# Prefix products by one scan, weight parts by copies and adding transfers, and a new order of all engines in a fused Mamba-2 and SiLU kernel

## The chip, the core and the metric

The kernel runs on one core of one Trainium2 chip. The engines of the core each work through their own queue in order: PE multiplies matrices (PEld loads the weights that stand in it), DVE is the vector engine, ACT the scalar engine, POOL the general one, and SP issues most of the DMA transfers; ACT and POOL can issue transfers too. The metric is the device time of one execution in microseconds (us), the median of several runs.

## What is computed

An attention block of the Mamba-2 kind for 4 batches, 8 heads, 768 positions, head dimension 32 and state size 16, and behind it a feed-forward block on its 3072 rows of 256 numbers:

```python
cum = np.cumsum(log_a[chunk])                       # log_a = log(clip(a))
L = np.exp(cum[:, None] - cum[None, :]) * causal    # decay between positions
y_intra = ((C @ B.T) * L) @ x                       # per chunk and head
y_inter = (C @ state) * np.exp(cum)
state = np.exp(cum[-1]) * state + (B * np.exp(cum[-1:] - cum)).T @ x
...
x = y.transpose(0, 2, 1, 3).reshape(3072, 256)
h = x @ w_in                                        # 256 x 2048
g = h * (1.0 / (1.0 + np.exp(-h)))
out = g @ w_out                                     # 2048 x 256
```

Everything is float32.

## The kernel before

**Tiling.** The positions are cut into 12 units of 256 (three for each batch), a unit into four chunks of 64. Two units make a group of 512 rows, 0 to 5. W_in and W_out are cut into 16 blocks of 256: blocks 0 to 7 are columns of W_in, block 8 + i holds the rows of W_out that belong to block i.

**Order.** Nothing is scheduled by a program: `SCHEDULE` is a long list of tokens written out by hand. A token such as `q,1,4,1,1` is a name with its arguments; the table `DO` maps the name to a function that records one step, and the loop at the end of the kernel runs the tokens one after the other. Each engine gets its instructions in the order of the list. `SLOTS` says, in the same way by hand, which buffer of the pools s2k (128 x 512), r4k (128 x 1024), raw (128 x 1024) and hp (matrix results) each new tile takes.

**Weights.** `lw,n` loads block n (512 KB, L288). ACT makes `u` and `v` of it (L294, L297), DVE does three bit operations `w,n,0` to `w,n,2` (L303, L307, L310), and POOL adds the two into the block `W` (L318). In group 0 the blocks 0 to 5 of W_in (`s`, L696) and all of W_out (`n1`, L760) are multiplied in plain float32. All else uses three float32r parts: high `H` (ACT, L322), low `lD` = H + W (DVE, L326), third `dD` = Z times H plus low (DVE, L330); the functions are `w_high`, `w_low` and `w_third`. The activations get three parts too: `xh`, `x,u,0`, `x,u,1` for W_in and `h`, `l`, `e` for W_out. Matmuls of W_in are `a` (high and low, 8 matmuls) and `d` (third part, 4; both L799), those of W_out `q` (3; L781), with `q,P,i,k,m` for group P, block 8 + i, half k of its rows and half m of the columns.

**Attention.** For a unit: `E` forms the decays by two scans (DVE, L511), `T` transposes C or B (DVE, L524; for units 0 and 1 `tp` on PE, L530, does a part), `ce` splits C by odd and even heads with the mask `par` (ACT, L545), `B` and `C` scale B and C (POOL, L519 and L550; `C,1` and `C,2` on DVE), `g0` (L584) and `gd` (L570) multiply, `M` masks (DVE, L599), `b` copies (ACT, L593), `S` and `SM` carry the state (DVE L612 and L614, ACT L622), `Y` multiplies (PE, L634 and L643), `y` copies, `xh` and `x` split. `par` is made by `cP`, two reductions of a constant (DVE, L419). Units 0 and 1 get their a, decays and prefix products from small loads of their own (`ia`, `ip`, `P01`, `as`, `ab`).

**Prefix products.** `C` and `S` need, for each chunk, the running product of a with a 1 in front, 65 numbers for each of 8 heads. For units 2 to 11 `ir` loads all of a (48 chunks as partitions), `AA` clips it on POOL into `azt` and `acp`, `AD,4` writes azt to DRAM as `az` (L465) and `AD,0` to `AD,3` write acp to DRAM as `ac`, one batch each (L467). `La` reads az back, spread for the decays (ab). `Lp,u` reads ac back, spread over 16 partitions a head, into `pz` (L237), and `P,u` makes the products of it with one DVE scan (L483) into `pfx`.

**Names in the profile.** Tiles keep the program's names: s2k and r4k are the pools; ga and gb are the two matrix result buffers of attention and of `a` and `d`; hp and o_ps are the others; raw also holds the split activations of groups 1 to 5.

Of the kernel before, what the change touches and what calls it, by code (L numbers as in the profile page):

```python
# [28 lines left out]
Ln,2,1,1,0 ir,2 w,11,0 AA,0 tp,2 AD,4 H,7 lD,7 u,8 lw,13 w,8,0 w,8,1 u,13 w,13,0 lw,6 u,15 H,3 Lt,3,0,0,0 u,6 w,6,0
w,13,1 H,2 s,1,4 w,15,0 w,15,1 s,0,1 si,0,1 s,1,0 AA,1 W,8 si,1,0 ce,2,1 Lt,3,1,1,0 w,11,2 a,0,7 v,6 w,11,1 AD,0 AD,1  # L30
w,9,2 dD,7 n1,1,1 ax,0,7 w,6,1 lw,10 s,0,2 w,6,2 v,15 u,10 w,15,2 d,0,7 si,0,2 W,11 lw,12 H,11 v,12 Lx,2,0,0 Lt,3,1,3,0
T,3,1 n1,0,0 v,13 n1,1,0 n1,6,1 La,2,1,0 dg,0,7 tq,2 La,2,0,0 E,2,1 W,15 w,10,0 n1,7,1 n1,15,1 n1,14,1 E,2,0 B,2 Lp,2,0
P,2 u,12 w,12,0 w,12,1 ce,2,0 Lt,3,0,2,0 g0,2 M,2,1 Lt,4,1,3,0 v,10 La,3,1,0 Lx,2,1,0 gd,2 n1,6,0 b,2,1 M,2,0 lw,14
n1,14,0 W,9 W,6 n1,2,0 w,13,2 Lt,3,0,1,0 n1,3,1 Lt,4,1,1,0 ce,3,1 H,5 Lx,3,0,0 H,9 b,2,0 S,2,0 S,2,1 S,2,2 ce,3,0 H,1
SM,2,1 n1,7,0 n1,15,0 C,2 u,14 SM,2,0 Y,2 La,3,0,0 E,3,0 W,13 v,14 si,1,4 w,10,2 y,2,0 Lt,4,1,2,0 H,6 E,3,1 Lt,3,0,3,0
T,3,0 Ln,3,0,1,0 Lx,3,1,0 Lp,3,0 P,3 n1,2,1 Ln,3,0,0,0 B,3 gd,3 w,12,2 W,12 Lt,4,0,0,0 lD,6 y,2,1 xh,2 g0,3 M,3,0 b,3,1
C,3 b,3,0 n1,10,1 n1,3,0 a,0,6 w,10,1 W,10 Lt,4,0,3,0 lD,0 S,3,0 S,3,1 M,3,1 dD,6 n1,11,0 H,13 S,3,2 Lp,4,0 w,14,0
Lt,4,1,0,0 w,14,1 Lx,4,1,0 ax,0,6 n1,10,0 x,2,1 H,15 SM,3,0 d,0,6 w,14,2 H,8 n1,5,0 La,4,1,0 n1,9,0 x,2,0 lD,5 La,4,0,0
E,4,0 Ln,4,0,1,0 dg,0,6 SM,3,1 Y,3 y,3,1 y,3,0 xh,3 lD,3 W,14 H,14 n1,13,0 n1,12,0 T,4,1 ce,4,0 n1,5,1 lD,9 n1,9,1 x,3,0
a,1,0 ax,1,0 n1,13,1 dD,5 Lt,4,0,2,0 x,3,1 n1,8,1 Lt,4,0,1,0 T,4,0 lD,1 ce,4,1 S,3,3 dD,0 d,1,0 P,4 C,4 n1,11,1 E,4,1  # L40
dg,1,0 lD,8 n1,12,1 dD,8 H,10 Lt,5,0,1,0 g0,4 Lx,4,0,0 Ln,4,0,0,0 B,4 H,4 gd,4 b,4,0 dD,1 M,4,1 b,4,1 S,4,0 S,4,1 S,4,2
SM,4,1 n1,4,0 M,4,0 Lt,5,1,1,0 SM,4,0 lD,4 Lt,5,1,0,0 lD,2 S,4,3 dD,2 h,1,0 dD,3 l,1,0 e,1,0 n1,8,0 n1,4,1 Vn,0 lD,10
Y,4 y,4,0 n1,0,1 y,4,1 a,1,1 xh,4 dD,10 H,12 lD,12 Vn,1 Lt,5,0,0,0 ax,1,1 a,1,2 ax,1,2 Lt,5,1,2,0 d,1,1 dg,1,1
Ln,5,0,0,0 Lt,5,1,3,0 T,5,1 La,5,1,0 o,0,0,2 q,1,0,0,1 La,6,1,0 ce,5,1 La,5,0,0 Ln,5,0,1,0 d,1,2 dg,1,2 h,1,2 ce,5,0
Lt,6,1,2,0 a,1,3 ax,1,3 q,1,0,1,1 a,1,4 ax,1,4 d,1,3 dg,1,3 Lp,5,0 q,1,0,1,0 E,5,1 E,5,0 B,5 o,0,1,2 lD,13 AD,2 lD,11
dD,4 Lx,5,0,0 l,1,2 e,1,2 d,1,4 dg,1,4 q,1,2,1,0 q,1,0,0,0 Lt,5,0,2,0 Lt,5,0,3,0 T,5,0 lD,15 dD,12 g0,5 x,4,1 Lx,5,1,0
Ln,6,0,0,0 gd,5 P,5 M,5,1 h,1,4 h,1,1 l,1,4 q,1,2,0,1 a,1,5 q,1,2,1,1 e,1,4 q,1,4,0,1 q,1,2,0,0 La,6,0,0 b,5,0 S,5,0
AD,3 Lt,6,1,1,0 q,1,4,0,0 b,5,1 ax,1,5 d,1,5 Ln,6,0,1,0 S,5,1 S,5,2 SM,5,0 M,5,0 SM,5,1 dD,13 Lt,6,1,3,0 x,4,0 q,1,4,1,1
q,1,4,1,0 C,5 dD,9 dg,1,5 h,1,5 Y,5 Lp,6,0 y,5,1 l,1,1 y,5,0 e,1,1 q,1,1,1,1 a,1,7 O,0,0,2,1,0 l,1,5 Lt,6,1,0,0
q,1,1,0,1 q,1,1,0,0 ax,1,7 e,1,5 d,1,7 Lt,6,0,0,0 xh,5 q,1,5,1,0 E,6,1 Lx,6,0,0 q,1,5,0,1 dg,1,7 Lt,6,0,3,0 T,6,1 ce,6,1  # L50
P,6 x,5,0 ce,6,0 Lt,6,0,2,0 Lt,6,0,1,0 T,6,0 q,1,5,0,0 E,6,0 h,1,7 C,6 g0,6 B,6 M,6,1 Lx,6,1,0 gd,6 b,6,0 Lt,7,1,2,0
h,1,3 q,1,1,1,0 S,6,0 M,6,0 dD,15 b,6,1 q,1,5,1,1 a,2,1 ax,2,1 S,6,1 S,6,2 SM,6,1 a,1,6 ax,1,6 l,1,7 e,1,7 q,1,7,0,0
q,1,7,0,1 d,1,6 dD,11 x,5,1 Lt,7,0,1,0 q,1,7,1,1 q,1,7,1,0 dg,1,6 d,2,1 l,1,3 e,1,3 lD,14 q,1,3,0,0 h,1,6 Lt,7,1,3,0
q,1,3,0,1 SM,6,0 l,1,6 dg,2,1 h,2,1 Y,6 La,7,1,0 y,6,0 e,1,6 Lt,7,1,0,0 Lx,7,1,0 S,6,3 Lt,7,1,1,0 T,7,1 ce,7,0 y,6,1
xh,6 Lt,8,1,0,0 q,1,3,1,1 dD,14 a,2,0 ax,2,0 q,1,6,1,0 q,1,6,1,1 ce,7,1 q,1,6,0,0 l,2,1 d,2,0 Ln,7,0,0,0 dg,2,0 h,2,0
Lp,7,0 P,7 O,0,1,2,0,0 e,2,1 q,1,6,0,1 x,6,1 Va,1,1 x,6,0 q,1,3,1,0 Lt,7,0,2,0 Vd,1,1 o,1,1,2 Lx,7,0,0 a,2,3 ax,2,3
Va,1,0 Vd,1,0 a,2,2 Lt,7,0,3,0 q,2,1,0,1 q,2,1,0,0 l,2,0 o,1,0,2 e,2,0 ax,2,2 d,2,2 q,2,1,1,0 d,2,3 q,2,0,0,0 dg,2,3
q,2,0,1,1 dg,2,2 h,2,2 q,2,1,1,1 La,7,0,0 E,7,0 Lt,7,0,0,0 O,0,1,2,2,0 O,0,0,2,3,0 q,2,0,0,1 C,7 T,7,0 g0,7 Ln,7,0,1,0
# [829 lines left out]
```

## Time and profile before

| | |
|---|---|
| median of 3 runs | 332.9 us (332.66 to 333.52) |
| the profiled execution's own time | 333.58 us |
| its span, first to last instruction | 331.8 us |
| mean granted clock of PE | 0.985 |
| DRAM read and written | 22.81 MB, 3.34 MB |
| instructions on PE, DVE, ACT, POOL | 3078, 350, 309, 64 |

The profile is one execution. Its page gives the busy time of each engine, the chain of work that ended last, and groups of instructions by source line (L12 is line 12); a row of a group reads: line, engine, operation, tile written <- tiles read, shapes, how many, then busy time in us and the mean of one in ns, then idle time ahead of them with what ended it. A row of the timeline begins with its start and its length in us, and its bracket names the wait ahead of it. A row of the windows reads: stretch, length, busy time (and number of instructions) of PE, PEld, DVE, ACT and POOL, granted clock (1.00 is full), share of the DMA engines, GB/s. A row of DMA issues ends with the size of one in KB and the median time from issue to landing in us.

### The profile page before, as it was taken

The numbers are of one execution on the slowest core, as the hardware profiler recorded it, in microseconds if no ns is written. First come the engines' busy times: TensorE is split into PE (matmuls) and PEld (weight loads), VectorE is DVE, ScalarE is ACT, GpSimd is POOL, SyncE is SP. The second block draws the span as 40 slices with busy tenths as digits, with TensorE's granted clock in tenths as the row PEclk, the third lists the DMA queues.
The fourth block names the chain that finished last, engine by engine and source line by source line (L and its number), as shares of the span: only waits on it lengthen the run. The fifth ranks groups of instructions, "written<-read, shape, count | busy, mean of one in ns | idle before, by whom it ended". The sixth has DMA issues, their size and how long they took to land.

```text
span 331.8 us, 7522 instructions
## 1 busy us (share of the span) xinstructions
PE 321.9 (97%) x3078; PEld 244.0 (74%) x3078; DVE 250.8 (76%) x350; ACT 204.9 (62%) x309; POOL 48.6 (15%) x64
## 2 busy tenths in 40 slices
...
GB/s 173 218 276 256 173 202 197 63 94 34 69 117 69 73 48 21 53 109 123 29 38 152 73 89 30 38 111 2 2 9 70 58 2 0 2 54 18 2 0 63
DMA packets 93522, 26.64 MB, mean 80 GB/s; under 512 B 79840, under 2 KB 86752, under 8 KB 93488
## 3 DMA queue, kind: packets, MB, share of 16 engines
...
q0 software_dynamic: 176, 0.20, 0.3%
...
HBM read 22.81 MB, written 3.34 MB: 79 GB/s over the span
## 4 chain that ended last, share of the span: by engine, by line
PE 78%; DVE 12%; DMA 4%; ACT 2%; issue 1%; SPq 1%; POOL 1%; DVEq 0%; POOLq 0%
PE hp L781 27%; PE ga L799 15%; PE gb L799 15%; PE o_ps L781 5%; PE hp L696 5%; PE hp L760 3%; DVE ab L511 3%; PE ga L634 2%; PE ga L584 2%; PE ga L643 1%; DVE ab L599 1%; DMA bn<-in_B_dram 1%; DVE s2k L330 1%; DVE s2k L326 1%; DMA tbc<-in_C_dram 1%
## 5 line engine op out<-in xcount | busy, mean ns | idle before, releaser
L781 PE MATMUL hp<-r4k,s2k 128*128 128x512 f32 x400 | 109.5, 394 | 0.0
L781 PEld LDWEIGHTS hp<-r4k,s2k 128*128 128x128 f32 x400 | 74.0, 188 | 16.4 <-issue 0.5
L650 DVE SCALAR_TENSOR_TENSOR r4k<-r4k,r4k 128x1024 fp32r<-128x1024 f32 (+1 forms) x42 | 50.4, 1199 | 36.6 <-ACT r4k L826 28.9
L799 PE MATMUL ga<-raw,s2k 128*128 128x512 f32 x240 | 62.1, 394 | 0.0
L799 PE MATMUL gb<-raw,s2k 128*128 128x512 f32 x240 | 62.0, 393 | 0.1
L799 PEld LDWEIGHTS gb<-raw,s2k 128*128 128x128 f32 x240 | 44.5, 188 | 11.6 <-ACT gb L810 1.2
L799 PEld LDWEIGHTS ga<-raw,s2k 128*128 128x128 f32 x240 | 44.6, 188 | 11.3 <-ACT ga L810 1.2
L836 DVE SCALAR_TENSOR_TENSOR r4k<-r4k,r4k 128x1024 fp32r<-128x1024 f32 x40 | 48.7, 1222 | 4.9 <-PE o_ps L781 1.5
L826 ACT ACTIVATE r4k<-r4k 128x1024 fp32r<-128x1024 f32 x40 | 41.9, 1057 | 2.0 <-PE hp L781 0.5
L810 ACT ACTIVATE ga<-ga 128x1024 f32<-128x1024 f32 x21 | 21.2, 1009 | 20.5 <-PE ga L799 20.5
L820 ACT ACTIVATE r4k<-gb 128x1024 f32<-128x1024 f32 x21 | 21.5, 1025 | 15.6 <-PE gb L799 15.4
L810 ACT ACTIVATE gb<-gb 128x1024 f32<-128x1024 f32 x21 | 21.2, 1008 | 15.6 <-PE gb L799 15.6
L820 ACT ACTIVATE r4k<-ga 128x1024 f32<-128x1024 f32 x21 | 21.5, 1024 | 15.0 <-PE ga L799 13.8
L781 PE MATMUL o_ps<-r4k,s2k 128*128 128x512 f32 x80 | 30.7, 390 | 0.0
L760 PE MATMUL hp<-r4k,s2k 128*128 128x512 f32 x64 | 30.1, 602 | 0.0
L318 POOL TENSOR_TENSOR s2k<-s2k,s2k 128x512 uint32<-128x512 uint32 (+1 forms) x19 | 24.1, 1280 | 22.6 <-DVE s2k L310 13.7
L519 POOL TENSOR_TENSOR BT<-bn,ab 128x256 f32<-128x256 f32 x10 | 7.3, 730 | 120.3 <-DVE ab L511 87.5
L511 DVE TENSOR_TENSOR_SCAN ab<-ab,diag 128x512 f32<-128x512 f32 x20 | 24.8, 1246 | 0.0
L696 PE MATMUL hp<-r4k,s2k 128*128 128x256 f32 x96 | 22.9, 395 | 0.0
L696 PEld LDWEIGHTS hp<-r4k,s2k 128*128 128x128 f32 x96 | 18.7, 199 | 3.4 <-issue 0.4
L760 PEld LDWEIGHTS hp<-r4k,s2k 128*128 128x128 f32 x64 | 11.6, 189 | 10.8 <-issue 9.3
L599 DVE TENSOR_TENSOR ab<-gb,ab 128x512 f32<-128x512 f32 x12 | 8.2, 686 | 12.3 <-PE gb L584 7.4
...
## 6 DMA issues: line engine op xcount, KB each, us to landing
ab<-az SPq DMA_DIRECT2D x20, 256.0 KB, 4.2
...
```

Source lines behind the costliest of these rows:

```text
L318: nc.gpsimd.tensor_tensor(out=u[:, :, fs], in0=u[:, :, fs], in1=v[:, :, fs], op=ALU.add)
L511: nc.vector.tensor_tensor_scan(out=o, data0=src, data1=diag.rearrange("p h t -> p (h t)"), initial=0.0, op0=ALU.mult, op1=ALU.add)
L599: nc.vector.tensor_tensor(out=o, in0=DP[u][w][:, :, 0:256].rearrange("p g (k x) -> p k g x", k=2), in1=o, op=ALU.mult)
L650: nc.vector.scalar_tensor_tensor(out=l, in0=f32(h), scalar=BACK, in1=y, op0=ALU.mult, op1=ALU.add)
L696: nc.tensor.matmul(out=hp[:, i], lhsT=WT[j][:, kc, 128 * i:128 * i + 128], rhs=XM()[:, 2 * kc:2 * kc + 2, u], start=(kc == 0), stop=(kc == ...
L760: nc.tensor.matmul(out=NP[m], lhsT=WT[8 + f // 2][:, f % 2, 128 * m:128 * m + 128], rhs=GT[0, f // 2][:, f % 2], start=(n == 1), stop=(n = ...
L781: nc.tensor.matmul(out=ACC[P, c], lhsT=WK[8 + i, p][:, k, 128 * m:128 * m + 128], rhs={"h": HT, "l": LT, "d": DT}[p][P, i][:, k], start=(n ...
L799: nc.tensor.matmul(out=o, lhsT=WK[j, q][:, kc, 128 * i:128 * i + 128], rhs=xs[:, 2 * kc:2 * kc + 2], start=(start and q == "h" and kc == 0 ...
L810: nc.scalar.activation(t, t, AF.Copy, scale=1.0 + Z)
L820: nc.scalar.activation(g, t, AF.Silu, scale=BACK)
L826: nc.scalar.activation(t, GT[G, i], AF.Copy, scale=-LESS * Z)
L836: nc.vector.scalar_tensor_tensor(out=DT[G, i], in0=f32(HT[G, i]), scalar=-1.0, in1=f32(LT[G, i]), op0=ALU.mult, op1=ALU.subtract)
```

## The change

Four things change.

1. **Prefix products.** The ten scans `P,u` go. One new step `AP` scans acp in place, for all units at once, 48 partitions by 8 x 65 = 520 elements, ahead of `AD,0` to `AD,3`, so that these write products; `Lp,u` loads them straight into `pfx`. The constant `one` of that scan takes a held r4k buffer in place of a tile of its own.
2. **Low parts.** Of the W_out blocks 10 to 15, `lD,n` is replaced by `Wl,n`, a copy of H on ACT (L335), and `Wm,n`, a transfer on POOL's queue that adds W onto the copy (256 KB, from one buffer to another). The functions `w_part` and `w_more` stood in the kernel before, unused.
3. **Third parts.** Of the W_out blocks 12 to 15, `dD,n` is replaced by `Wd,n`, a copy of H times Z on ACT, and `We,n`, a transfer that adds the low part.
4. **Order.** `SCHEDULE` and `SLOTS` are written anew as a whole; the number of tokens is 1289 in both. Counts of the steps: `P` 10 to 0, `AP` 0 to 1, `lD` 16 to 10, `dD` 16 to 12, `Wl` and `Wm` 0 to 6, `Wd` and `We` 0 to 4, idle matmuls `z` 17 to 16; all others as before.

The functions `w_part` and `w_more`, the same in both:

```python
def w_part(n, p):
    t = WK[n, p] = small(f"{p}{n}", [128, 2, WF], FR)
    nc.scalar.activation(t, f32(WK[n, "h"]), AF.Copy, scale=1.0 if p == "l" else Z)

def w_more(n, p):
    other = WT[n] if p == "l" else f32(WK[n, "l"])
    nc.gpsimd.dma_start(out=f32(WK[n, p]).rearrange("p k f -> p (k f)"),
                        in_=other.rearrange("p k f -> p (k f)"), accum_op=ALU.add)
```

The start of the order, and the stretch with the last adding transfers:

```diff
-cp cI c1 lw,4 ci z,1 z,1 z,1 z,1 ia,0 ct v,4 ia,1 z,1 z,1 z,0,6 z,1 cd ip,0,0 z,1 co u,4 ca A AT AU as,1,0 lw,0 ir,0 z,1
-as,0,0 ab,0,0 ch P01,0,0 P01,0,1 w,4,0 E,0,0 Lt,0,1,2,0 z,1 Lt,0,1,1,0 Ln,0,0,1,1 Ln,0,0,0,1 B,0,0 z,0,6 z,0,6 as,0,1
-ab,0,1 z,0,6 v,0 w,0,2 Lt,0,1,0,0 Lt,0,1,3,0 T,0,1 C,0 Ln,1,0,0,0 ir,3 Lx,0,0,0 tp,0 as,1,1 Lx,0,1,0 ab,1,0 E,0,1 u,0
-w,0,0 w,0,1 tq,0 B,0,1 cP ce,0,1 lw,5 ce,0,0 E,1,0 Ln,1,1,0,0 z,1 W,0,1 D,0 S,0,0 v,5 W,0,0 B,1,0 S,0,1 S,0,2 SM,0,1
-z,0,6 g0,0 M,0,1 Lt,3,1,0,0 M,0,0 lw,3 u,5 SM,0,0 v,3 w,5,0 w,5,1 u,3 w,5,2 S,0,3 ab,1,1 E,1,1 Ln,1,1,1,0 Y,0 X0,0,1
-X0,0,0 w,3,0 xh,0 w,3,2 Ln,1,0,1,0 tp,1 tq,1 s,0,0 ip,1,0 P01,1,0 Lx,1,1,0 w,4,1 w,3,1 ce,1,1 W,5 Lx,1,0,0 ce,1,0 si,0,0
...
+ci z,1 c1 z,1 z,1 Ln,0,0,1,1 ch z,0,6 cd ct cI ia,0 z,1 ia,1 ip,0,0 cp z,0,6 ip,1,0 z,0,6 ca A AT AU Ln,0,0,0,1 z,0,6
+as,0,1 ab,0,1 as,1,1 z,0,6 as,0,0 ab,0,0 P01,0,0 P01,0,1 P01,1,0 E,0,1 B,0,1 lw,5 u,5 z,1 E,0,0 z,0,6 v,5 cP z,1
+Lt,0,1,3,0 w,5,0 Lt,0,1,0,0 Lt,0,1,2,0 Lt,0,1,1,0 T,0,1 Lx,0,0,0 tp,0 tq,0 B,0,0 w,5,1 w,5,2 P01,1,1 ab,1,1 Lx,0,1,0
+lw,0 D,0 W,5 S,0,0 ce,0,0 S,0,1 S,0,2 ce,0,1 g0,0 M,0,0 M,0,1 S,0,3 as,1,0 u,0 w,0,0 Ln,1,0,0,0 z,1 Ln,1,1,0,0 v,0 z,1
+z,1 w,0,2 SM,0,1 C,0 ab,1,0 w,0,1 W,0,0 SM,0,0 E,1,1 lw,4 u,4 Y,0 X0,0,0 X0,0,1 v,4 z,1 Ln,1,1,1,0 Ln,1,0,1,0 tp,1
+ce,1,1 W,0,1 ce,1,0 E,1,0 B,1,0 w,4,0 w,4,1 tq,1 C,1 lw,1 u,1 s,0,5 si,0,5 xh,0 w,4,2 g0,1 w,1,0 B,1,1 Lx,1,1,0 Lx,1,0,0
...
+M,5,0 Lt,6,1,1,0 h,1,5 q,1,1,0,1 T,6,1 l,1,4 q,1,3,1,0 Y,5 y,5,1 e,1,4 q,1,1,1,1 a,1,7 Wm,12 l,1,5 We,12 Wm,15 q,1,4,1,1
+ce,6,0 Lt,7,1,3,0 y,5,0 xh,5 q,1,3,0,0 x,5,1 Lx,7,0,0 Ln,6,0,1,0 ce,6,1 ax,1,7 d,1,7 dg,1,7 q,1,4,0,1 E,6,0 q,1,4,0,0
+Lt,6,0,1,0 T,6,0 x,5,0 g0,6 h,1,7 Ln,6,0,0,0 B,6 M,6,1 Lx,6,1,0 gd,6 b,6,0 b,6,1 M,6,0 S,6,0 Lp,6,0 S,6,1 S,6,2 S,6,3
+q,1,4,1,0 Wd,15 a,2,1 ax,2,1 a,1,6 d,2,1 ax,1,6 SM,6,0 e,1,5 l,1,7 q,1,3,0,1 dg,2,1 d,1,6 O,0,0,2,2,0 q,1,3,1,1 We,15
+e,1,7 q,1,7,1,1 La,7,0,0 SM,6,1 dg,1,6 h,1,6 l,1,6 e,1,6 C,6 Y,6 y,6,0 q,1,7,0,1 a,2,0 h,2,1 ax,2,0 q,1,7,0,0
...
```

On POOL's queue the new order has, around the transfers: `B,3`, `C,3`, `Wm,13`, `W,11`, `Wm,10`, `AD,3`, `Wm,11`, `B,4`, `AD,2`, `C,4`, `Wm,14`, `C,5`, `We,13`, `B,5`, `Wm,12`, `We,12`, `Wm,15`, `B,6`, `We,15`, `C,6`, `We,14`, `C,7`. `We,n` waits for the landing of `Wm,n`.

The functions:

```diff
-    one = const.tile([128, 4, Q + 1], FP32, name="one")
...
     def load_pz(u, q):
         q = QUEUES[q]
-        PZ[u] = keep("pz", [128, 4, Q + 1], loads)
+        PFX[u] = keep("pfx", [128, 4, Q + 1], loads2, u % 2)
...
-        q.dma_start(out=PZ[u].rearrange("p c t -> p (c t)"),
+        q.dma_start(out=PFX[u].rearrange("p c t -> p (c t)"),
...
+    def one():
+        return held("one", [NCH, H, Q + 1], key="r4k")
...
     def c_one():
-        nc.gpsimd.memset(one, 0.0)
-        nc.gpsimd.memset(one[:, :, 0:1], 1.0)
+        nc.gpsimd.memset(one(), 0.0)
+        nc.gpsimd.memset(one()[:, :, 0:1], 1.0)
...
-    def f_P(u):
-        PFX[u] = keep("pfx", [128, 4, Q + 1], loads)
-        nc.vector.tensor_tensor_scan(out=PFX[u].rearrange("p c t -> p (c t)"),
-                                     data0=PZ[u].rearrange("p c t -> p (c t)"),
-                                     data1=one.rearrange("p c t -> p (c t)"), initial=0.0,
+    def f_AP():
+        t = acp().rearrange("p h t -> p (h t)")
+        nc.vector.tensor_tensor_scan(out=t, data0=t, data1=one().rearrange("p h t -> p (h t)"), initial=0.0,
                                      op0=ALU.mult, op1=ALU.add)
...
-        "P01": f_P01, "P": f_P, "T": f_T, "tp": f_TP, "tq": f_TQ, "ce": f_T2, "B": f_B, "C": f_C,
+        "P01": f_P01, "AP": f_AP, "T": f_T, "tp": f_TP, "tq": f_TQ, "ce": f_T2, "B": f_B, "C": f_C,
```

The functions from `f_AP` on stand one line further down than in the kernel before.

More of the change, by code (lines that the diff above doesn't have):

```diff
@@ L29 @@
[L29 to L58, printed above, removed]
```

128 lines of the change are left out of this document (77 added, 51 removed), and 6 rows, old and new, of the table SLOTS.

## The prediction

> **What bounds the kernel now.** I read the page first (engine shares, the granted clock, the chain of waits), then the windows (busy time of PE, PEld, DVE, ACT, POOL; granted clock; DMA share; GB/s), then the timeline of the stretches in which PE is not full.
>
> ```profile
> PE 321.9 (97%) x3078; PEld 244.0 (74%) x3078; DVE 250.8 (76%) x350; ACT 204.9 (62%) x309; POOL 48.6 (15%) x64
> PE 78%; DVE 12%; DMA 4%; ACT 2%; issue 1%; SPq 1%; POOL 1%; DVEq 0%; POOLq 0%
> 0.00:20.00 20.00, 14.39 (x217) 8.63 (x217) 14.38 (x36) 10.57 (x21) 6.77 (x21) 0.80 0.82 193
> 20.00:328.00 308.00, 306.81 (x2856) 235.02 (x2855) 236.00 (x315) 193.98 (x288) 41.87 (x44) 1.00 0.32 73
> ```
> From 20 us to 328 us PE is busy 306.81 of 308.00. The change leaves PE's matmuls as they are, apart from their order, so work taken from DVE there is worth nothing by itself. Time can be won ahead of 20 us, in the last 3.8 us, or in the part of the 308 that isn't matmul pace. The first is where to look:
>
> ```profile
> 0.81 0.45 SPq L288 DMA_DIRECT2D raw<-in_moe_w_in_dram  x1
> 1.32 1.61 SPq L372 DMA_DIRECT2D s2k<-in_a_dram  x2
> 4.54 0.21 DVE L445 TENSOR_SCALAR s2k<-s2k 32x128 f32<-32x128 f32 x1 [1.61 <-DMA s2k<-in_a_dram]
> 9.69 0.69 DVE L310 SCALAR_TENSOR_TENSOR s2k<-raw,s2k 128x512 uint32<-128x512 uint32 x1 [0.75 <-ACT s2k L297]
> 10.30 0.64 DVE L524 STREAM_TRANSPOSE ct<-s2k 128x256 f32<-128x256 f32 x1
> 10.78 1.16 DVE L511 TENSOR_TENSOR_SCAN ab<-hp,diag 128x512 f32<-128x512 f32 x1
> 13.15 0.21 DVE L419 TENSOR_REDUCE par<-hm 128x1 f32<-128x4 f32 x2
> 13.40 0.91 ACT L545 ACTIVATE ce<-ct,par 128x256 f32<-128x256 f32 x2 [1.29 <-DVE par L419]
> 16.30 0.68 DVE L599 TENSOR_TENSOR ab<-ga,ab 128x512 f32<-128x512 f32 x1
> 19.09 1.11 PE L530 MATMUL o_ps<-ident,s2k 128*128 128x128 f32 x4
> 19.99 3.03 PE L696 MATMUL hp<-r4k,s2k 128*128 128x256 f32 x8
> ```
> SP issues a 512 KB weight block ahead of the loads of a; DVE waits until 4.54 for them. C's transpose `T,0,1` ends at 10.94, but ACT's `ce` waits until 13.40 for `par`, two reductions (`cP`, L419) that depend on nothing late: they merely stand behind a scan and two weight operations on DVE. Then g0, the masks `M` (end 16.98), Y, and at 19.99 the first W_in matmul.
>
> **The change part by part.**
>
> *Head.* The new order puts `cP` ahead of `T,0,1`, puts `lw,4` and two raw-a loads behind the first loads, and starts with `s,0,5`. Ahead of the end of `T,0,1` DVE gains the second scan of unit 0 (1.16), `cP` (0.21) and one clamp of L472 (0.28) and loses the operation of L310 (0.69) with its wait of 0.75 us for v: +0.96, less 0.1 as neighbouring records overlap by some hundredths. The a loads come 0.50 earlier (the L288 issue goes). 10.94 + 0.86 − 0.75 − 0.50 = 10.55. `ce`, g0 and M follow as before (16.98 − 13.40 = 3.58 us), so M ends near 14.1 instead of 17.0: 2.9 us earlier, and the first s at about 17.1. The transposes L530 waited until 19.09 for a B load of unit 1, the last of which is now issued behind three weight blocks instead of four and without the raw-a loads, so I let them follow. The clock decides how much of the 2.9 is kept:
>
> ```profile
> 16.00:18.00 2.00, 1.44 (x32) 0.95 (x31) 1.97 (x5) 1.70 (x4) 0.00 (x0) 0.50 0.86 157
> 20.00:22.00 2.00, 2.00 (x6) 1.64 (x6) 2.00 (x6) 1.51 (x4) 0.50 (x2) 0.50 1.04 360
> 22.00:24.00 2.00, 2.00 (x69) 1.29 (x68) 0.74 (x3) 0.94 (x2) 1.38 (x1) 0.95 1.08 299
> 17.13 0.37 PE ga L634 x2
> ```
> The granted clock is 0.50 while matmuls are sparse and is back at 0.95 from about 22.2, some 5.1 us after the dense matmuls begin with Y,0 at 17.13. If the clock comes back the same 5.1 us after a dense start at 14.2, the whole 2.9 is kept. If it stays at 0.50 until 22.2 whatever PE does, work brought forward runs at half pace and half is kept, 1.45. I take 2.3, nearer the first, since PE has no gap behind Y,0 in either order.
>
> [...]
>
> *DVE.* Removed: ten scans (L483), six low parts (L326), four third parts (L330). Added: one scan of 520 elements, by its nearest row (L511).
>
> ```profile
> L472 DVE TENSOR_SCALAR s2k<-s2k 128x256 f32<-128x256 f32 x2 | 0.6, 283 | 0.0
> L483 DVE TENSOR_TENSOR_SCAN pfx<-pz,one 128x260 f32<-128x260 f32 x10 | 7.2, 716 | 2.5 <-DMA pz<-ac 2.5
> L326 DVE TENSOR_TENSOR s2k<-s2k,s2k 128x512 fp32r<-128x512 f32 x16 | 13.2, 836 | 0.6 <-ACT s2k L322 0.6
> L330 DVE SCALAR_TENSOR_TENSOR s2k<-s2k,s2k 128x512 fp32r<-128x512 f32 x16 | 12.2, 771 | 0.1
> L511 DVE TENSOR_TENSOR_SCAN ab<-ab,diag 128x512 f32<-128x512 f32 x20 | 24.8, 1246 | 0.0
> L322 ACT ACTIVATE s2k<-s2k 128x512 fp32r<-128x512 f32 x16 | 9.8, 626 | 0.0
> 20.00:77.40 57.40, 56.78 (x636) 38.01 (x636) 52.48 (x86) 41.27 (x82) 27.69 (x26) 0.98 0.63 172
> 77.40:128.00 50.60, 50.48 (x553) 37.09 (x552) 48.13 (x70) 31.82 (x49) 6.54 (x8) 1.00 0.34 71
> ```
> DVE gets 7.2 + 6 × 0.836 + 4 × 0.771 − 1.25 = 14 us less, ACT 10 × 0.626 = 6.3 us more. ACT is 72% busy (41.27 of 57.40), then 63%, so its part is covered by idle time, and so is DVE's saving: PE is full in both windows. Value 0. But DVE is near its limit up to 128 us (52.48 of 57.40, 48.13 of 50.60), and the order decides when its saving comes:
>
> ```profile
> 68.76 0.68 DVE L599 TENSOR_TENSOR ab<-gb,ab 128x512 f32<-128x512 f32 x1
> 73.00 0.27 PE L634 MATMUL ga<-cw,sm 32*64 32x64 f32 x2
> 77.23 0.66 DVE L650 SCALAR_TENSOR_TENSOR raw<-raw,ys 128x512 fp32r<-128x512 f32 x1
> 77.44 2.41 PE L799 MATMUL ga<-raw,s2k 128*128 128x512 f32 x8
> ```
> Unit 3's last M ended at 69.44 and was used by Y,3 at 73.00, 3.6 us later. In the new order 107 instead of 102 DVE instructions stand ahead of it: two scans of L483 and two weight operations gone (2.1 us net of overlaps), AP, two low and two third parts, three bit operations and a state update come (5.0): 2.9 us later in the queue, while PE is 2.3 us earlier. 3.6 − 2.9 − 2.3 = −1.6: here up to 1.6 us of the head's gain may be given back. `x,3,0` ended at 77.89, with a,1,0 already started on the halves that were ready, so it has no slack; 113 instead of 115 instructions, 1.2 us less, stand ahead of it, which leaves 1.1 of the 2.3 uncovered. But DVE itself starts earlier, by some 0.5 to 2 us, as its first 20 us held waits (busy 14.38 of 20.00). Bounds of this loss 0 and 1.6; I take 0.2, since DVE's early start answers most of it. Everything later is relieved.
>
> *Transfers.* Ten 256 KB adding transfers on POOL's queue; no such transfer is in the trace. Nearest rows of issue (mean ns) and of landing (us):
>
> ```profile
> L467 POOL DMA_DIRECT2D ac<-r4k x4 | 2.8, 696 | 0.0
> ac<-r4k POOLq DMA_DIRECT2D x4, 24.4 KB, 3.8
> az<-s2k POOLq DMA_DIRECT2D x1, 96.0 KB, 2.8
> ab<-az SPq DMA_DIRECT2D x20, 256.0 KB, 4.2
> 115.98 1.99 PE L799 MATMUL gb<-raw,s2k 128*128 128x512 f32 x8
> 117.81 0.62 PE L781 MATMUL hp<-r4k,s2k 128*128 128x512 f32 x2
> 119.17 1.14 PE L799 MATMUL gb<-raw,s2k 128*128 128x512 f32 x4
> 120.14 1.30 PE L781 MATMUL hp<-r4k,s2k 128*128 128x512 f32 x5
> L519 POOL TENSOR_TENSOR BT<-bn,ab 128x256 f32<-128x256 f32 x10 | 7.3, 730 | 120.3 <-DVE ab L511 87.5 <-PE gb L799 18.9 <-DMA tbc<-in_B_dram 13.9
> ```
> Ten issues are 7 us of a POOL that is busy 6.54 of the 50.60 us in which they mostly fall: hidden. Landing takes 2.8 at least; 4.2 for as many bytes; 8.4 if adding reads and writes twice. I take 5. PE paces 8 matmuls in 1.83 us (115.98 to 117.81), 4 in 0.97, 3 in 0.7.
> - `We,15` waits for ACT's copy `Wd,15`, queued behind `b,6,1` and so behind gd,6 on PE, and done about 1.2 us after gd,6. From gd,6 to q,1,7,1,1, which reads the sum, PE has two a (8), two d (4) and three q (3): 3.66 + 1.94 + 2.1 = 7.7 us. Less 1.2 and the issue of 0.7: it decides from 5.8 us.
> - `We,12` waits on POOL for the landing of `Wm,12`, issued behind `B,5`. From x,3,0 to the scan that B,5 needs, DVE has 35 instructions of 48.13/70 = 0.69, 24.1 us; from a,1,0 to q,1,4,1,1, which needs both, PE has seven a, six d and 13 q (12.8 + 5.8 + 9.1) and nine n1 and two each of g0, gd and Y (some 13.1 by their spacing in the trace), 40.8. So 16.7 − 0.73 (B,5) − 2 × 0.7 = 14.5 for two landings: it decides from 7.2 us each. `B,6` is queued behind We,12 and `Wm,15`, `C,6` behind We,15; gd,6 and Y,6 wait for these, but come later than the q named.
>
> At 5 us nothing waits: value 0. At 8.4: 8.4 − 5.8 = 2.6 and 2 × 1.2 = 2.4, together 5.0 us lost.
>
> *Scan first, then dump.* Lp,2 waits for `AP`, then AD,0's landing (3.8 by the four ac dumps), then its own load (~4). AP stands near 44 us, so this ends near 53, where DVE's C,2 arrives at about 52.5: 0 to 0.5 us on DVE, within the loss above.
>
> *Tail.* The same last steps in a slightly other order: 0, bounds ±0.3.
>
> Sum: −2.3 + 0.2 = −2.1. The profiled execution's 331.8 us span becomes 329.7; with the 1.8 outside it (333.58 in all), 331.5. The median of the runs shown is 332.9, 0.7 less, so I take the gain from it: 330.8.
>
> **The rivals.**
> 1. The head's gain is eaten by DVE at Y,3 or a,1,0. For: DVE's 52.48 of 57.40 and the count of 2.9 us. Against: its waits before 20 us. With 1.6 lost and only 1.45 won by the clock, 333.0; with 1.6 of 2.3, 332.2: no change.
> 2. Slower: the adding transfers land late, at `We,15` and at the pair `Wm,12`, `We,12`, in PE's queue at q,1,7,1,1 and q,1,4,1,1. It decides from 5.8 and 7.2 us, and outweighs the head from 7.4 (1.6 + 0.4 = 2.0). [...] Against: 4.2 for as many bytes that come from DRAM. Price at 8.4: 5.0 − 2.1 = +2.9, 335.8; at 7.5 it is +0.2, 333.1; the middle is 334.5.
> 3. More: PE's losses inside the 308 us go too. PE's order is new throughout; the matmuls at their paces add up to about 6 us less than 308 takes. A third to a half of that besides: 328.3.
> 4. The order doesn't help the head: the weight loads ahead of unit 1's B still hold PE until 19. Then 332.9, no change.
> 5. POOL's issues grow while DVE is full. An issue longer by s makes We,15 late from s = 5.8 − 5 = 0.8 and the pair from (14.5 − 10)/2 = 2.2; at s = 2 that is 1.2 us, 332.0, no change. Against: the four of L467 took 696 ns in the mean with DVE near its limit. [...]
>
> **How the numbers follow.** Forecast 0.54 (own range 329.3 to 332.0); rivals 1 and 4 0.15; rival 5 0.04; rival 2 0.20; rival 3 0.07. About 0.3%, 1 us, is what a measurement tells from no change. Faster: 0.54 + 0.07 less 0.02 for the forecast's upper edge, 0.59; same 0.15 + 0.04 + 0.02 = 0.21; slower 0.20. The range reaches from 328.3 (rival 3) into rival 2, 334.5.
>
> **What would show it.** Right: `ce` starts near 10.6 and no longer waits for par, the first L696 near 17, the clock back before 20; the issues of `Wm` and `We` (L339) at 0.7 and landings near 5 us; PE without a wait on them. Wrong: idle PE ahead of Y,3 or a,1,0 released by DVE; PE waiting for a DMA at q,1,4,1,1 or q,1,7,1,1; L696 at 19 or later behind a B load.

## The result and the profile after

The prediction was faster, 330.8 us. The changed kernel takes 335.41 us (median of 7 runs, 334.39 to 336.15); the kernel before takes 332.66 beside it (7 runs, 331.17 to 333.52). The ratio is 1.0088 with a 95% interval of 1.006 to 1.0116: 2 to 4 us slower. The profiled execution of after took 335.41, its span is 333.7 us, against 333.58 and 331.8 before.

The page (engine shares, chain of waits) and the windows of after, in the same stretches as before:

```profile
PE 320.6 (96%) x3074; PEld 244.6 (73%) x3077; DVE 241.5 (72%) x331; ACT 209.6 (63%) x319; POOL 58.6 (18%) x74
PE 75%; DVE 9%; SPq 6%; DMA 5%; issue 1%; ACT 1%; DVEq 0%
```

```profile
0.00:20.00 20.00, 14.77 (x221) 10.21 (x225) 14.81 (x37) 10.05 (x21) 7.10 (x19) 0.95 0.74 165
20.00:77.40 57.40, 54.60 (x630) 36.68 (x629) 51.10 (x81) 42.69 (x85) 27.91 (x28) 0.99 0.72 181
77.40:128.00 50.60, 50.13 (x548) 36.13 (x547) 45.25 (x64) 35.44 (x56) 14.63 (x18) 1.00 0.66 125
128.00:328.00 200.00, 199.89 (x1674) 161.03 (x1673) 129.06 (x147) 120.99 (x159) 8.98 (x11) 1.00 0.25 44
```
DVE is busy 9.3 us less (14 was forecast; operations that stayed took longer, the 16 of L310 888 ns in the mean instead of 726), ACT 4.7 more (6.3), POOL 10.0 more (7). Between 20 and 77.4 us PE is now idle 2.80 us (57.40 − 54.60) where it was idle 0.62; from 77.4 on the two are alike (0.47 and 0.11 idle, before 0.12 and 0.46). In the chain of waits SP's queue has gone from 1% to 6%. So most of the time went before 77.4 us, and the place to look is what PE waits for there. The timeline of after, head:

```profile
11.25 0.91 ACT L546 ACTIVATE ce<-ct,par 128x256 f32<-128x256 f32 x2 [0.35 <-DVE ct L525]
15.19 0.27 PE L635 MATMUL ga<-cw,sm 32*64 32x64 f32 x2 [0.92 <-ACT sm L623]
18.08 0.90 PE L531 MATMUL o_ps<-ident,s2k 128*128 128x128 f32 x3 [1.09 <-DMA s2k<-in_B_dram]
18.77 3.14 PE L697 MATMUL hp<-r4k,s2k 128*128 128x256 f32 x8
23.20 0.56 PE L571 MATMUL hp<-s2k,BT 64*32 64x64 f32 x32 [0.66 <-DMA s2k<-in_x_dram]
```
`ce` is 2.15 us earlier than before and no longer waits for par. But PE then waits for a B load of unit 1 until 18.08, so the first s comes at 18.77, 1.2 us earlier and not 2.9, and at 23.20 it waits for x of unit 1.

SP's queue and the work of unit 3, some 40 us later:

```profile
57.14 0.42 SPq L254 DMA_DIRECT2D bn<-in_B_dram  x1
64.22 0.33 SPq L262 DMA_DIRECT2D tbc<-in_C_dram  x1
64.59 0.43 SPq L254 DMA_DIRECT2D bn<-in_B_dram  x1
65.07 0.58 SPq L269 DMA_DIRECT2D xt<-in_x_dram  x1
68.24 0.62 SPq L237 DMA_DIRECT2D pfx<-ac  x1
63.55 0.65 DVE L525 STREAM_TRANSPOSE ct<-tbc 128x256 f32<-128x256 f32 x1
63.62 0.70 PE L761 MATMUL hp<-r4k,s2k 128*128 128x512 f32 x1 [0.64 <-POOL s2k L318]
70.54 0.46 PE L571 MATMUL ga<-xt,BT 64*32 64x64 f32 x32 [0.99 <-DMA xt<-in_x_dram]
74.29 0.27 PE L635 MATMUL ga<-cw,sm 32*64 32x64 f32 x2 [0.51 <-DVE ab L600]
```
SP issues nothing from 57.56 to 64.22, 6.7 us. The load that ends the gap is `Lt,4,1,2`, C of unit 4. Units 2 to 11 share one `tbc` buffer, and T,3,1 on DVE (63.55 to 64.20; the row that writes `ct`) is what reads unit 3's C from it. The expectations below call it T,3,0, which is B's transpose and comes after it. Behind that load in the queue stand the second half of unit 3's B, its x and its products: 64.59, 65.07, 68.24. PE waits for x at gd,3 (0.99) and for M at Y,3 (0.51). In the kernel before, C's transpose T,3,1 stood 15 us earlier on DVE, at 48.5 us, so no load of unit 4's C waited for it here. Two loads of unit 4's B, Lt,4,0,0 and Lt,4,0,3, did wait for T,3,0, but stood behind unit 3's B, x and products (SP's timeline of before):

```profile
56.19 0.38 SPq L269 DMA_DIRECT2D xt<-in_x_dram  x1
56.80 1.25 SPq L237 DMA_DIRECT2D pz<-ac  x1
58.49 0.37 SPq L254 DMA_DIRECT2D bn<-in_B_dram  x1
62.79 0.80 SPq L262 DMA_DIRECT2D tbc<-in_B_dram  x2
```

The adding transfers, by the DMA issues (KB each, median us to landing) and by the view of their line (ns, least, median and most; then who waited for them):

```profile
s2k<-s2k POOLq DMA_DIRECT2D x10, 256.0 KB, 4.1
```

```profile
L339 POOL DMA_DIRECT2D s2k<-s2k x10: 854/880/1196, 72.5 to 127.0; - x10
  POOL s2k L339: 3.5, 1
```
They land in 4.1 us, and none but the We,12 behind Wm,12 waits for one; PE doesn't.

### The profile page after: what moved, and what is told of

Its sections match the earlier page's. It is cut to its first block, busy times and chain, and to the rows that moved or that the text cites. A ratio compares the mean times of both kernels' runs of the same rounds, so it can differ in the third digit from the quotient of the medians.

```text
span 333.7 us, 7536 instructions
## 1 busy us (share of the span) xinstructions
PE 320.6 (96%) x3074; PEld 244.6 (73%) x3077; DVE 241.5 (72%) x331; ACT 209.6 (63%) x319; POOL 58.6 (18%) x74
## 4 chain that ended last, share of the span: by engine, by line
PE 75%; DVE 9%; SPq 6%; DMA 5%; issue 1%; ACT 1%; DVEq 0%
PE hp L782 28%; PE gb L800 16%; PE ga L800 16%; PE o_ps L782 5%; PE hp L697 3%; DVE s2k L310 2%; DMA s2k<-in_x_dram 2%; DMA raw<-in_moe_w_in_dram 2%; SPq L262 2%; PE ga L635 1%; SPq L254 1%; DVE ab L512 1%; PE ga L644 1%; PE ga L585 1%; SPq L288 1%
## 5 line engine op out<-in xcount | busy, mean ns | idle before, releaser
L520 POOL TENSOR_TENSOR BT<-bn,ab 128x256 f32<-128x256 f32 x10 | 8.7, 867 | 84.0 <-DVE ab L512 57.5
L551 POOL TENSOR_TENSOR cw<-ct,pfx 128x256 f32<-128x256 f32 x9 | 8.3, 926 | 70.7 <-PE gb L635 46.6
```

Of the source, the lines that this page charges most:

```text
L520: nc.gpsimd.tensor_tensor(out=BT[u][:, ks], in0=bn[u][:, ks], in1=E[u][:, ks, :, Q - 1:Q].to_broadcast([128, n, H, N]), op=ALU.mult)
```

## The experiments

Each ran for five rounds beside the kernel before, and the ratio is to that; its median was 332.5 to 333.7 us in the four groups, so ratios are compared, not times. Line numbers in these kernels are a few lower than in after.

| kernel | what it changes | ratio | 95% interval |
|---|---|---|---|
| after | | 1.0088 | 1.006 to 1.0116 |
| a_sp3 | after, three loads moved | 1.0029 | 1.0004 to 1.0054 |
| a_head | after, two weight loads moved | 1.0089 | 1.0054 to 1.0125 |
| a_sp3_head | both | 1.0034 | 1.0012 to 1.0057 |
| a_dve | after, no adding transfers | 1.0185 | 1.014 to 1.023 |
| a_best1 | a_sp3, PE and ACT reordered in the head | 1.001 | 0.9988 to 1.0031 |
| b_sp3 | before, two loads moved | 1.0243 | 1.0203 to 1.0282 |
| b_cp | before, cP moved | 0.998 | 0.996 to 1.0001 |
| b_tr | before, adding transfers alone | 1.0339 | 1.03 to 1.0377 |
| b_ap | before, one scan alone | 1.011 | 1.0082 to 1.0139 |
| b_ap2 | b_ap, dumps later | 1.0157 | 1.0105 to 1.0209 |
| b_best | b_cp and more | 1.0055 | 1.003 to 1.008 |
| b_best2 | b_best mended | 1.0006 | 0.9984 to 1.0029 |

**a_sp3: unit 4's loads behind unit 3's.**

```diff
-... Ln,3,0,1,0 u,11 n1,1,1 Lt,4,1,2,0 E,3,0 Ln,3,0,0,0 E,3,1 B,3 n1,11,0 ce,3,1 Lx,3,1,0 Lt,4,1,0,0 Lt,4,0,1,0 g0,3 ...
+... Ln,3,0,1,0 u,11 n1,1,1 E,3,0 Ln,3,0,0,0 E,3,1 B,3 n1,11,0 ce,3,1 Lx,3,1,0 g0,3 ...
...
-... Wl,10 Lp,3,0 C,3 ...
+... Wl,10 Lp,3,0 Lt,4,1,2,0 Lt,4,1,0,0 Lt,4,0,1,0 C,3 ...
```

> The kernel after with three loads moved on SP's queue: the loads of C and B of unit 4 (Lt,4,1,2 Lt,4,1,0 Lt,4,0,1) stand behind the loads of unit 3 (Ln,3,0,0 Lx,3 Lp,3). Theory 1 (SP): in the profile of after SP issues nothing from 57.56 to 64.22, since Lt,4,1,2 overwrites the one tbc buffer that T,3,0 on DVE reads until 64.2; x, B and the products of unit 3 come 8 to 12 us late, and PE waits 1.0 us at gd,3 and 0.5 at Y,3. Then those loads issue by 60 us, both waits go, and the time falls by 1.5 us from 335.4 to about 333.9. Theory 2 (DVE's queue is late and would hold Y,3 in any case): gd,3 no longer waits but Y,3 waits as much longer, gain under 0.5 us, 335.0 or more. Theory 3 (the adding transfers cost the time): no change, 335.4.

1.0029: two thirds of the loss are gone, about 2 us. SP's timeline of a_sp3 shows why:

```profile
57.00 1.04 SPq L251 DMA_DIRECT2D bn<-in_B_dram  x2
58.08 3.11 SPq L266 DMA_DIRECT2D xt<-in_x_dram  x2
61.82 0.61 SPq L234 DMA_DIRECT2D pfx<-ac  x1
63.13 0.80 SPq L259 DMA_DIRECT2D tbc<-in_C_dram  x2
```
Both halves of B are issued by 58.04 and x by 61.2; the tbc load still doesn't start before 63.13, but no load of unit 3 is behind it. PE's wait at gd,3 is gone and that at Y,3 is 0.32 us. Theory 1 holds; theory 3 (the transfers) falls.

**b_sp3: the same fault put into the kernel before.**

```diff
-... T,3,0 Ln,3,0,1,0 Lx,3,1,0 Lp,3,0 P,3 n1,2,1 Ln,3,0,0,0 B,3 gd,3 w,12,2 W,12 Lt,4,0,0,0 ...
+... T,3,0 Lt,4,0,0,0 Lt,4,0,3,0 Ln,3,0,1,0 Lx,3,1,0 Lp,3,0 P,3 n1,2,1 Ln,3,0,0,0 B,3 gd,3 w,12,2 W,12 ...
```

> The kernel before with the fault put in: two of unit 4's loads (Lt,4,0,0 and Lt,4,0,3, which overwrite the one tbc buffer once T,3,0 has read it) ahead of unit 3's loads of B, x and products on SP's queue. Theory 1: SP holds them back until DVE has done T,3,0 (62.8 in the profile of before), unit 3's loads come 5 to 8 us later, PE waits for x or for M at unit 3, and the time rises by 1 to 2 us, ratio 1.003 to 1.006. If the order of these loads doesn't matter: 1.000.

1.0243, far more than expected. SP and PE in its timeline:

```profile
53.82 9.46 SPq L254 DMA_DIRECT2D tbc<-in_B_dram  x3
63.77 0.39 SPq L246 DMA_DIRECT2D bn<-in_B_dram  x1
69.57 0.68 PE L562 MATMUL ga<-xt,BT 64*32 64x64 f32 x32 [6.78 <-POOL BT L511]
```
Two loads in front of others cost 6.8 us of PE here, since B,3 on POOL and gd,3 on PE wait for B; in after other matmuls stood ahead of gd,3 in PE's order. The matmuls behind the wait ran slower as well: the 32 of gd,3 took 0.68 us instead of 0.46 in before, and the mean granted clock of this execution was 0.973, against 0.985 in before's. With a_sp3 this settles the mechanism from both sides.

**a_head and a_sp3_head: weight loads behind unit 1's B and x.** Blocks 4 and 1 are loaded later, and what ACT and DVE do with them stands later too.

```diff
-... lw,4 u,4 Y,0 X0,0,0 X0,0,1 v,4 ... tp,1 ce,1,1 W,0,1 ce,1,0 E,1,0 B,1,0 w,4,0 w,4,1 tq,1 C,1 lw,1 u,1 s,0,5 si,0,5 xh,0 w,4,2 g0,1 w,1,0 B,1,1 Lx,1,1,0 Lx,1,0,0 D,1 ...
+... Y,0 X0,0,0 X0,0,1 ... tp,1 ce,1,1 W,0,1 ce,1,0 E,1,0 B,1,0 tq,1 C,1 s,0,5 si,0,5 xh,0 g0,1 B,1,1 Lx,1,1,0 Lx,1,0,0 lw,4 lw,1 D,1 S,1,0 u,4 M,1,1 v,4 w,4,0 ...
```

> The kernel after with the loads of weight blocks 4 and 1 behind the loads of B and x of unit 1 on SP's queue, and the operations on these blocks on ACT, DVE and POOL moved behind with them. Theory: after won only 1.2 us in the head (first s at 18.77 instead of 19.99), because the transposes waited until 18.08 for a B load of unit 1 and the state of unit 1 until 23.20 for x, both behind 512 KB blocks while the DMA engines are full (share 1.0). Then the transposes start near 17, the first s near 17.7, the clock may not fall to 0.5 at 17.9, and the waits of 1.09 and 0.66 us go: 334.2, 1.2 us less. Rival (the weight blocks 4 and 1 are then late by as much): PE waits for W,4 at s,0,4 for 1 us or more, no gain or a loss of up to 1 us, 335.4 to 336.4.

> The kernel after with both moves on SP's queue (unit 4's loads behind unit 3's; blocks 4 and 1 behind unit 1's B and x). If the two losses are separate and both theories hold, the gains add: 335.4 - 1.5 - 1.2 = 332.7, equal to before. If DVE's queue sets the time between 60 and 76 us, the head's gain is lost there again: as a_sp3, about 333.9 to 335.

1.0089 and 1.0034: nothing, with or without the other move. PE's waits in the head of a_sp3_head:

```profile
15.14 0.27 PE L630 MATMUL ga<-cw,sm 32*64 32x64 f32 x2 [0.91 <-ACT sm L618]
25.48 3.78 PE L692 MATMUL hp<-r4k,s2k 128*128 128x256 f32 x8 [3.53 <-POOL s2k L313]
```
The waits for B and x are gone and one of 3.53 us for the weights of block 4 has come; the eight matmuls behind it took 3.78 us, where eight of the same line took 1.99 at 19.95, and the granted clock was 0.91 in the mean from 20 to 60 us, against 1.00 in a_sp3. The rival held: in the head of after the DMA engines are full (share 0.99 to 1.09 from 18 to 24 us), and with B and x brought forward block 4 came late.

**a_best1: other PE work ahead of the loads.** a_sp3, and in the head the loads as in after, but s,0,5 and s,0,0 ahead of what waits for B and x.

```diff
-... M,0,1 S,0,3 as,1,0 u,0 ... SM,0,1 C,0 ab,1,0 w,0,1 W,0,0 SM,0,0 E,1,1 lw,4 u,4 Y,0 X0,0,0 X0,0,1 v,4 z,1 ... tp,1 ... tq,1 C,1 lw,1 u,1 s,0,5 ... g0,1 ... D,1 ... u,7 v,7 Ln,2,1,1,0 s,0,0 SM,1,0 SM,1,1 ...
+... ce,0,1 as,1,0 SM,0,1 SM,0,0 g0,0 ... M,0,1 S,0,3 u,0 ... lw,4 Y,0 X0,0,0 X0,0,1 u,4 v,4 z,1 ... W,0,1 s,0,5 si,0,5 tp,1 ... tq,1 C,1 lw,1 s,0,0 ... g0,1 ... D,1 ... SM,1,0 SM,1,1 u,7 v,7 ...
```

> The kernel after with unit 4's loads behind unit 3's on SP (as in a_sp3) and, in the head, with the loads left as they are but PE's and ACT's order changed: the first two s (s,0,5 and s,0,0) ahead of the transposes of unit 1, which wait for a B load, and of its state, which waits for x; the copies X0 and the state masks SM,0 and SM,1 ahead of the weight operations that wait for 512 KB blocks. Theory: a_sp3 still loses 0.9 us to the B load, 1.3 to x and 0.9 to SM at the head, all of it in front of work that is ready; it then goes, and PE stays dense, so that the clock doesn't fall: 1.5 to 3 us under a_sp3, ratio to before 0.994 to 0.998, faster than before. Rival (DVE's queue sets the pace from 40 us on, so that what is won in the head is lost at Y,3 and Y,4): as a_sp3, 1.003.

1.001: another 0.2% by the middle of the intervals, which overlap; equal to before, not faster. In its timeline and windows:

```profile
16.30 1.99 PE L689 MATMUL hp<-r4k,s2k 128*128 128x256 f32 x8 [0.34 <-ACT r4k L658]
25.68 0.27 PE L627 MATMUL ga<-cw,sm 32*64 32x64 f32 x2 [1.22 <-DVE ab L592]
20.00:77.40 57.40, 53.96 (x626) 35.04 (x625) 54.51 (x83) 43.77 (x86) 29.72 (x30) 1.00 0.76 188
```
The first s comes at 16.30, 3.7 us earlier than in before's profile, and runs at full clock (1.99 us for eight instead of 3.03). But PE is then idle 3.44 us of the 57.40, and DVE is busy 54.51: what the head wins waits again for DVE, first at Y,1. The expected rival, in part.

**b_cp: the prediction's head step alone.**

```diff
-... Lt,0,1,3,0 T,0,1 C,0 ... tq,0 B,0,1 cP ce,0,1 ...
+... Lt,0,1,3,0 cP T,0,1 C,0 ... tq,0 B,0,1 ce,0,1 ...
```

> The kernel before with one step moved: cP (par) ahead of T,0,1 on DVE. The prediction's step: ce waits for par until 13.40, and 2.3 to 2.9 us are to be had by it. That step alone: ce from about 11.2, Y,0 from about 15, first s from 18, ratio 0.994. Theory now: the transposes ahead of the first s wait for a B load of unit 1 until 19.09, so ce's wait cost nothing: first s at 19.9 again, ratio 1.000 within 0.002.

0.998, between the two expectations. ACT's and PE's rows:

```profile
12.27 0.90 ACT L537 ACTIVATE ce<-ct,par 128x256 f32<-128x256 f32 x2
16.48 0.27 PE L626 MATMUL ga<-cw,sm 32*64 32x64 f32 x2 [1.12 <-ACT sm L614]
18.64 1.96 PE L688 MATMUL hp<-r4k,s2k 128*128 128x256 f32 x8 [0.21 <-issue]
```
`ce` comes 1.1 us earlier and not 2.2 (ACT first does `tq,0`, which waits 1.29 us for PE), Y,0 0.65 (it now waits for SM). B's load isn't the limit in this order: the transposes of unit 1 follow Y,0 without a wait for it (PE):

```profile
17.77 0.66 PE L522 MATMUL o_ps<-ident,s2k 128*128 128x128 f32 x4
```
The step is worth about 0.2%, not 0.7%, and the interval just takes in nothing at all.

**b_best and b_best2: more of the head in the old order.** SM,0, X0 and M,0 ahead of the work on blocks 5 and 3 and of the scan E,1,0; in b_best2 the transposes ab,1,1 behind Y,0.

```diff
-... ce,0,0 E,1,0 ... v,5 W,0,0 B,1,0 S,0,1 S,0,2 SM,0,1 z,0,6 g0,0 M,0,1 ... M,0,0 lw,3 u,5 SM,0,0 v,3 ... u,3 w,5,2 S,0,3 ab,1,1 E,1,1 ... Y,0 X0,0,1 X0,0,0 w,3,0 ...
+... ce,0,0 ... W,0,0 S,0,1 S,0,2 SM,0,1 SM,0,0 z,0,6 g0,0 M,0,1 ... M,0,0 E,1,0 B,1,0 lw,3 v,5 u,5 ... w,5,2 S,0,3 ... Y,0 ab,1,1 E,1,1 X0,0,1 X0,0,0 v,3 u,3 w,3,0 ...
```

> The kernel before with cP ahead of T,0,1 (as in b_cp) and, in the head, the state masks SM,0, the copies X0 and the masks M,0 ahead of the operations on weight blocks 5 and 3 on ACT and of the scan E,1,0 on DVE. Theory: in b_cp Y,0 waited 1.12 us for SM and the first s came at 18.64; DVE and PE are ready by 15.1; so Y,0 at 15.3 or so, first s near 17.5, another 1 us: ratio 0.995 (0.993 to 0.997), faster than both kernels. Rival (the transposes then wait for their B load, or the weights of the second s are late): as b_cp, 0.998.

> b_best with what went wrong in it mended: there the transposes ab,1,1, ahead of Y,0 on PE, waited 2.74 us for the moved scan E,1,0, which frees their buffer; now they and their scan stand behind Y,0. Theory: Y,0 no longer waits for SM or for E,1,0 and comes near 15.4, first s near 17.5 against 18.64 in b_cp: ratio 0.995 (0.993 to 0.997), faster than before and after. Rival (the transposes of unit 1 then wait for their B load, or E,1,1 is late for Y,1, or what is won there is lost to DVE's queue by 77 us): as b_cp, 0.998 or more.

Both theories missed; of b_best2 the rival's number, 0.998 or more, came. In b_best ab,1,1 waited on PE ahead of Y,0 for the moved scan, which frees its buffer:

```profile
16.83 0.63 PE L494 MATMUL hp<-ident,s2k 128*128 128x128 f32 x4 [2.74 <-DVE ab L504]
```
b_best2 has no such wait and is still 1.0006. In its profiled execution PE waits ahead of Y,0 for the masks M instead, and the clock fell in the head (timeline, windows):

```profile
17.09 0.37 PE L627 MATMUL ga<-cw,sm 32*64 32x64 f32 x2 [1.61 <-DVE ab L592]
12.00:14.00 2.00, 1.76 (x42) 0.95 (x41) 1.69 (x4) 1.18 (x3) 1.64 (x4) 0.81 1.11 284
16.00:18.00 2.00, 0.91 (x32) 0.82 (x38) 2.00 (x4) 0.69 (x2) 0.00 (x0) 0.50 0.32 77
```
Y,0 comes at 17.09 and not near 15.4. A sparser PE ahead of Y,0 and a lower clock go together here; that the one brought the other in the timed runs is not shown: the mean granted clock of the 12 executions has a median of 0.9935, that of the 17 of before beside them 0.993.

**a_dve and b_tr: the transfers, taken out and put in.** a_dve has lD in the place of Wm and dD in that of We, and no copies; b_tr has Wl, Wm in the place of lD and Wd, We in that of dD, in the old order.

```diff
-... H,12 Wd,12 ... H,13 Wl,13 ... Wm,13 ... Wl,12 ... Wm,12 ... We,12 ...
+... H,12 ... H,13 ... lD,13 ... lD,12 ... dD,12 ...
```

```diff
-... lD,10 ... dD,10 H,12 lD,12 ... lD,15 dD,12 ...
+... Wl,10 Wm,10 ... dD,10 H,12 Wl,12 Wm,12 ... Wl,15 Wm,15 Wd,12 We,12 ...
```

> The kernel after without copies and adding transfers: the six low and four third parts are made by DVE (as in the kernel before), at the places of the transfers in the order; everything else as after. Theory 1 (the new order of loads on SP costs the time, the transfers nothing): the transfers land in 4.1 us, and PE waits for none; without them DVE has some 8 us more work behind 72 us, where it has idle time: no change, 335.4 within 0.7. Theory 3 (the transfers cost the time, by landings or by load on the DMA engines): 332.7 to 333.5. If DVE is still near its limit there, slower than 336.

> The kernel before with the copies and adding transfers alone: for the same six and four blocks Wl, Wm in the place of lD and Wd, We in the place of dD, all else in the old order. DVE has 8 us less work, behind 75 us. Prediction's step: transfers that land in about 4 us are hidden, DVE's saving is worth nothing: 1.000 within 0.002. Rival: in the old order the parts come just in time for their matmuls, so that PE waits for some transfers: 1.003 or more. If the saving on DVE were worth time by itself (as a_dve against after suggests), under 0.997.

Both are slower, 1.0185 and 1.0339, and both theories that gave the transfers no weight missed; the rivals, slower than 336 us and 1.003 or more, came. The waits of a_dve (two rows) and of b_tr (two rows):

```profile
PE hp L755 <- issue: 2.5, 1, 2.5
PE o_ps L776 <- DVE s2k L324: 1.2, 2, 1.0
```

```profile
PE hp L779 <- DMA s2k<-s2k: 4.1, 1, 4.1
PE o_ps L779 <- DVE s2k L328: 2.4, 1, 2.4
```
In a_dve PE waits 1.2 us for third parts that DVE makes. A full DVE is not enough to explain it: DVE is busy 47.58 of 50.60 us from 77.4 to 128 there, but in the kernel before it was busy 48.13, and PE was idle 0.12. Another 2.5 us of a_dve have no shown cause (the last section), so how much of its 1% over after the ten parts cost is open. In the old order a part made by copy and transfer in the place of one made by DVE comes late for its q, and PE waits 4.1 us for one. So the transfers and the new order belong together as they are placed here: the order alone costs 1.9%, the transfers alone 3.4%, both together 0.9%.

**b_ap and b_ap2: one scan alone.** In the old order the ten P go, two scans of four heads each make the products in place, and Lp loads them into two pfx buffers; in b_ap2 the dumps AD,0 and AD,1 stand behind W,11 on POOL.

```diff
-... Lt,3,1,1,0 w,11,2 a,0,7 v,6 w,11,1 AD,0 AD,1 ... Lp,2,0 P,2 ...
+... Lt,3,1,1,0 AP w,11,2 a,0,7 v,6 w,11,1 AD,0 AD,1 ... Lp,2,0 ...
```

> The kernel before with the prefix products alone changed: two scans over acp (four heads each, with the constant of before) ahead of AD,0 in place of the ten scans P, loads straight into pfx with two buffers. DVE has 6 us less work, two instructions less ahead of unit 3's M. Both theories: the loads of products wait for the scan and the dump (some 3 to 5 us later for unit 2), Y,2 is needed at 62, so no change, ratio 0.998 to 1.001. If the scan ahead of the dump costs time: PE waits ahead of Y,2 or gd,3, and 1.002 or more.

> b_ap with the two dumps AD,0 and AD,1 behind W,11 on POOL instead of ahead of it. In b_ap POOL waited 3.26 us at AD,0 for the scan; W,11 behind it then ran 46.16 to 51.90 instead of 1.3 us, and PE waited 2.0 and 0.8 us for it. If what cost the 1.1% is the place of the wait on POOL's queue, 0.999 to 1.002 here. If the one scan (its dump and load chain) costs it by itself, 1.008 or more.

1.011 and 1.0157. POOL and PE in b_ap, by timeline and by the view of the line of W (least, median, most ns):

```profile
44.80 1.34 POOL L459 DMA_DIRECT2D ac<-r4k  x2 [3.26 <-DVE r4k L476]
46.16 6.98 POOL L310 TENSOR_TENSOR s2k<-s2k,s2k 128x512 uint32<-128x512 uint32 x2
51.95 1.98 PE L751 MATMUL hp<-r4k,s2k 128*128 128x512 f32 x4 [2.00 <-POOL s2k L310]
```

```profile
L310 POOL TENSOR_TENSOR s2k<-s2k,s2k x6: 1267/1277/5741, 40.1 to 59.5; 128x512 uint32<-128x512 uint32 x6
```
POOL waits 3.26 us for the scan, and the next W, started while DVE works without a gap, takes 5.7 us instead of 1.3; PE waits for it. Moving the dumps didn't help: in b_ap2 a W took 6.7. So what the scan costs by itself, without this long W, stays open; in after no W took over 1.66 us, and none of PE's waits listed above names AP or its loads.

## Why the prediction was wrong

- **"I let them follow" (the loads of unit 1).** This step failed. ce came earlier (11.25; 10.55 was forecast), but the transposes waited for B until 18.08 and unit 1's state for x until 23.20. The 2.9 us were 1.2 at the first s, and by 24 us nothing was left of them: PE's rows from there on add up to the same, 371.9 us before and 371.7 after (more than the span, since small matmuls overlap). The row of 19.09 in the prediction was misread too: it has no wait in its bracket. In before, the transposes followed Y,0 at half clock, and in b_cp, in the same order of loads, they began at 17.77 without a wait for B. The limit by B came with the new order, and the sum counted what stood ahead of T,0,1 on DVE and not when the loads land.
- **"Everything later is relieved" and "bounds of this loss 0 and 1.6; I take 0.2".** This is the larger failure. The place was right (unit 3), the mechanism not: DVE's instructions were counted, SP's queue past unit 3 was not. `Lt,4,1,2` stands ahead of unit 3's loads and waits for T,3,1, which the new order has 15 us later, since there is one tbc buffer. a_sp3 puts its price at 0.6% (1.0088 against 1.0029), b_sp3 shows the same fault in the other kernel. Rival 1 named Y,3 and priced the loss at 1.6 us; it had DVE as the cause. That the measured 335.41 lies within what rival 2 priced, 333.1 to 335.8, is luck: the late transfers that it names didn't come.
- **The clock.** The gain was to be kept to four fifths since PE is dense from Y,0 on. In after it wasn't dense: PE waited at 18.08, and the clock, full until 17.9, was 0.50 in the window from 18 to 20 us. The 0.50 that the prediction read in before was one execution's: after had no low clock to come back from when Y,0 began.

```profile
16.00:18.00 2.00, 0.82 (x55) 0.55 (x33) 2.00 (x3) 1.03 (x3) 1.42 (x2) 0.97 0.80 95
18.00:20.00 2.00, 1.92 (x6) 1.71 (x7) 1.24 (x3) 1.68 (x5) 1.00 (x2) 0.50 1.02 285
```
- **The transfers.** Landing (4.1 us; 5 was taken) and issue (0.88; 0.7 was taken) were near, and rival 2 didn't come. Its 8.4, a known landing doubled, is in no run: the ten landed in 3.3 to 5.5 us, where the 256 KB loads of ab took 4.2 in before. We,15 was issued 1.84 us after gd,6 (125.71 after 123.87) and its q began at 131.90: 8.0 us after gd,6, where 7.7 was forecast. What is in doubt is "value 0" for DVE's saving: without it, in a_dve, this order is 1% slower, of which 1.2 us are waits for the parts and the rest is open. A saving that PE's busy share hides can still matter to the order.
- **The issue rival (5).** Ten issues took 854 to 1196 ns with DVE busy 45.25 of 50.60 us: at most 0.5 us over the 0.7 taken, where the rival began to cost at 0.8. Its growth of 2 us is in no run.
- **Scan ahead of the dump** gave PE no wait in after. **The tail** was given ±0.3; from L727 (L726 before) to the end it took 4.7 us before and 5.3 after (328.42 to 333.7), 0.55 more in these two executions.

Together: the forecast was 2.1 us less and the runs gave 2.75 more. Of the 4.85 between them the head's gain that didn't stay is 2.3, SP's queue 1.8 (2.0 less the 0.2 that had been taken), the tail 0.55. The first and the last are read from one execution each, so this sum fits better than it can be trusted to.
